# One load of 128 rows issued as sixteen loads of 15, 14, 13, ... 1 and 8 rows

## The chip, the cores and the metric

The kernel runs on one core of a Trainium2 chip. The time is device microseconds for one execution of the program; the median of three runs is given. The profile is one other execution, taken by the hardware profiler.

## The reference

A decode step for four sequences (one new token each, width 576): layer norm, attention over the last 4096 positions of a key/value cache (32 query heads of width 128 on 16 key/value heads), output projection and residual; then layer norm, a gated MLP of width 4608 with a ReLU gate, and residual. All inputs and the output are bf16.

```python
def _A_ref(x, k_cache, v_cache, wq, wo):           # Hq = 32, Hkv = 16, Sk = 16384, Dh = 128
    W = min(4096, max(256, Sk // 4))
    q = (x @ wq).reshape(B, Sq, Hq, Dh).transpose(0, 2, 1, 3)
    k = jnp.repeat(k_cache[:, :, Sk - W:, :], rep, axis=1)
    v = jnp.repeat(v_cache[:, :, Sk - W:, :], rep, axis=1)
    p = softmax(jnp.einsum("bhqd,bhkd->bhqk", q, k) * Dh ** -0.5)
    o = jnp.einsum("bhqk,bhkd->bhqd", p, v)
    return o.transpose(0, 2, 1, 3).reshape(B, Sq, Hq * Dh) @ wo
def _B_ref(x, W_gate, W_up, W_down):               # W_gate, W_up: 576 x 4608, W_down: 4608 x 576
    gate, up = x @ W_gate, x @ W_up
    return (gate * (gate > 0) * up) @ W_down
h  = x + _A_ref(layernorm(x), ...)
h2 = h + _B_ref(layernorm(h), ...)
```

## The kernel before

The kernel is written engine by engine: each operation is put on the list of its engine by hand, with the operations that it depends on, and `Prog.emit` turns those into semaphore waits. An engine runs its list in order. All large loads are issued by SP (the sync queue), in the order of the program text; only the load of x and half of the output's store are issued by ACT.

**What is loaded, in order.** W_q (the last 64 of its 576 rows first, in one piece; then the other 512), then 16 K tiles and 16 V tiles of 4 MB each (one sequence and four key/value heads a tile), alternating from the fifth K tile on, then W_o, W_gate, W_up and W_down. The K and V tiles go through four slots of one big SBUF tensor, `arena`; the later weights are laid over the same space. `place` keeps, for each 64 columns of `arena`, which operation read them last (`owner`), and makes a load wait for that reader. So SP waits, before most loads, for matmuls that free the space. Each load has its own semaphore or that of its slot; a load adds 16 to it when it has landed in full.

**What is computed.** For each K tile: a transposition on DVE in place (L422), then the score matmuls on PE (L446 and, for those that reuse the loaded weights, the helper at L34). For each V tile: the matmuls of probabilities by values (L507, L34), and a selection of the wanted rows on ACT and DVE (L517, L520, L523, L524). After the last V tile: the output projection (L615, L34), the norm (L618 to L645), the gate and up matmuls (L664, L34), ReLU and product (L670, L673), a transposition (L677), the down matmuls (L685), two copies (L701, L702) and the store (L706).

**Around the change.** W_gate and W_up have 576 rows; 512 of them are loaded as 128 partitions of four rows each (`main_rows`), and the last 64 as 128 partitions of half a row each (`last_rows`): 2304 elements, 4608 bytes a partition. The loop at L268 to L277 issues, for W_gate, the last 64 rows (called part 4) at L276, then the 512 rows in one load; for W_up the last 64 rows, then three quarters of the others, then the last quarter. W_down comes in five pieces (L282) of 15, 10, 7, 3 and 1 of its 36 rows a partition. The load of W_gate's part 4 waits for nothing that the load of W_o before it did not wait for; the load after it waits for the matmuls of an earlier V tile. The gate matmuls (L664) read part 4 first.

```python
def last_rows(W):
    return W[512:576, :].rearrange("r (a n) -> (r a) n", a=2)
...
for g, W in ((0, B_W_gate), (1, B_W_up)):
    for m, n, src in ((4, F // 2, last_rows(W)), ...
        place(("gu", g, m), off, n, ("GU", g, m), lambda e, off=off, n=n, src=src: e.dma_start(out=arena[:, off:off + n], in_=src))
```

Of the kernel before, what the change touches and what calls it, by code (L numbers as in the profile page):

```python
# [120 lines left out]
def bass_sequential_preLN__sliding_block_cached__glu_gated_reglu__decode_kernel(  # L121
# [12 lines left out]
    with ExitStack() as es:  # L134
        cnt = [0]

        def sb(name, shape, dt):
            return es.enter_context(nc.sbuf_tensor("sb_" + name, shape, dt))

        P = Prog()  # L140
# [8 lines left out]
        arena = sb("arena", [128, AW], BF16)  # L149
# [66 lines left out]
        def place(name, off, size, reader, make, key=None):  # L216
            deps = []
            for blk in range(off // 64, (off + size) // 64):
                r = owner.get(blk)
                if r is not None and r not in deps:  # L220
                    deps.append(r)
                owner[blk] = reader
            semk = key or "d_" + "_".join(str(v) for v in name)
            P.dma("sync", ("L",) + name, make, semk, deps)
            land[name] = off

        ring = [(-1 - 2 * NTILE) % NSLOT]
# [7 lines left out]
        def add_kv(kind, g):  # L235
            b, qd = divmod(g, 4)
            s = ring_slot()
            off = slot0 + s * TILE
            cache = A_k_cache if kind == "K" else A_v_cache
            src = cache[b, 4 * qd:4 * qd + 4, SK - WIN:SK, :].rearrange("a (p t) d -> p a (t d)", p=32)  # L240
            place((kind, g), off, TILE, ("QK", g) if kind == "K" else ("PV", g),
                  lambda e: e.dma_start(out=arena[:, off:off + TILE], in_=src), key=f"slot{s}")  # L242


        def main_rows(W):
            return W[0:512, :].rearrange("(p r) n -> p (r n)", r=4)

        def last_rows(W):
            return W[512:576, :].rearrange("r (a n) -> (r a) n", a=2)

        P.dma("sync", ("L", "wq", 1), lambda e: e.dma_start(out=pT[:, 0:2048], in_=last_rows(A_wq)), "d_wq1")  # L251
        s = ring_slot()
        wq_off = slot0 + s * TILE
        place(("wq", 0), wq_off, TILE, "QMM",
              lambda e: e.dma_start(out=arena[:, wq_off:wq_off + TILE], in_=main_rows(A_wq)), key=f"slot{s}")  # L255
        for g in range(NTILE):
# [6 lines left out]
        for g in range(NTILE - 4, NTILE):  # L263
            add_kv("V", g)
        place(("wo",), WO_OFF, H * D, "WO",
              lambda e: e.dma_start(out=arena[:, WO_OFF:WO_OFF + H * D], in_=A_wo.rearrange("(p r) n -> p (r n)", p=128)))
        gu_off = {}
        off = WO_OFF + H * D  # L268
        for g, W in ((0, B_W_gate), (1, B_W_up)):
            for m, n, src in ((4, F // 2, last_rows(W)), (0, 3 * F, main_rows(W)[:, 0:3 * F]), (3, F, main_rows(W)[:, 3 * F:4 * F])):  # L270
                if g == 0 and m == 0:
                    n, src = 4 * F, main_rows(W)
                elif g == 0 and m == 3:
                    continue
                gu_off[(g, m)] = off
                place(("gu", g, m), off, n, ("GU", g, m), lambda e, off=off, n=n, src=src: e.dma_start(out=arena[:, off:off + n], in_=src))  # L276
                off += n  # L277
        WD_ROWS = (0, 15, 25, 32, 35, 36)
        wd_off = off
        for r0, r1 in zip(WD_ROWS, WD_ROWS[1:]):  # L280
            place(("wd", r0), wd_off + r0 * D, (r1 - r0) * D, ("DOWN", 1),
                  lambda e, r0=r0, r1=r1: e.dma_start(  # L282
                      out=arena[:, wd_off + r0 * D:wd_off + r1 * D],
                      in_=B_W_down.rearrange("(p r) n -> p (r n)", p=128)[:, r0 * D:r1 * D]))
# [18 lines left out]
                                                in_=c_qm[:, :, :].rearrange("p q (h j) -> p q h j", j=4),  # L303
# [4 lines left out]
                                                in_=to_v[:, :, :].rearrange("p n (k a) -> p n k a", a=4),  # L308
# [14 lines left out]
        for sg in range(2):  # L323
            pool(f"c_toq{sg + 1}", lambda e, sg=sg: e.affine_select(
                out=toq[:, :, :, :], in_=toq[:, :, :, :],
# [213 lines left out]
        def finish_o():  # L539
            for q in range(4):  # L540
                for qd in range(4):
# [17 lines left out]
                                              in_=bass.AP(tensor=e8, offset=0, ap=[[8, 128], [0, 4], [1, 8]])), ["c_e8", "c_selc0"])  # L559
# [47 lines left out]
        for a in range(8):  # L607
            for n in range(2):
                for j in range(4):
# [4 lines left out]
                    else:  # L614
# [6 lines left out]
                                             in_=bass.AP(tensor=psb, offset=512 + 224, ap=[[4096, 128], [1, 64], [0, 2]])), ["part1"])  # L621
# [27 lines left out]
        for g in range(2):  # L649
            for c in (4, 0, 1, 2, 3):  # L650
                part_ = c if c == 4 or (c == 3 and g) else 0
                for m in range(3):
                    for j in range(4):
                        first = m == 0 and j == 0 and (c in (0, 4) or part_ == 3)
                        deps = [("L", "gu", g, part_)] if first else []
# [20 lines left out]
        for i in range(2):  # L676
            dve(("HHT", i), lambda e, i=i: e.transpose(  # L677
                out=hhT[:, 576 * i:576 * i + 576].rearrange("p (r q) -> p r q", q=32),
                in_=bass.AP(tensor=pp, offset=3712 + 18 * i, ap=[[PPW, 128], [1, 18], [36, 32]])), [("HH", m) for m in range(3)])
# [12 lines left out]
        for r in range(36):  # L692
            for n in range(2):
                deps = []
# [9 lines left out]
        for n in range(2):  # L704
            lo, hi = ncol[n]
            P.dma(("sync", "scalar")[n], ("O", n), lambda e, n=n, lo=lo, hi=hi: e.dma_start(  # L706
                out=orow[:, lo:hi], in_=out_sb[32 * n:32 * n + 4, 0:hi - lo]),
# [31 lines left out]
```

## Time and profile before

| | |
|---|---|
| median of 3 runs | 378.08 us (378.05 to 378.56) |
| the profiled execution: its own time is its span, first to last instruction | 376.5 us |
| loaded from HBM | 159.58 MB, 424 GB/s over the span |
| busy | PE 209.2 us, DVE 227.6, ACT 53.8, POOL 10.7 |
| chain of waits, share by engine | DMA 62%, DVE 18%, PE 18% |
| granted TensorE clock, mean | 0.791 |
| W_gate's part 4: size; issue to landing | 576 KB; 27.2 us |

The profile's page gives busy times and shares of the span for each engine, the DMA queues with what they moved, and the chain of work that ended last. Queue 1 is SP's, queue 10 ACT's; queues 8 and 14 carry the program's instructions. The median of the runs is 1.6 us above the span of the profiled execution.

### The profile page before, as it was taken

What the parts mean: (1) busy time and instruction counts of PE and PEld (TensorE: products, weight loads), DVE (VectorE), ACT (ScalarE), POOL (GpSimd) and SP (SyncE); (2) the same over time, 40 slices, a digit from 0 to 9 for tenths busy, and PEclk for the clock granted to TensorE, in tenths of its full rate; (3) what the DMA queues carried; (4) which work ended last, traced back from release to release, by engine and by line L of the source; (5) the groups of instructions that cost most, each with busy time, mean ns of one, the idle gap of its engine ahead of it and who ended that gap; (6) DMA issues with size and microseconds to landing.
All of it is one profiled execution on the core that took longest, in us unless ns stands there. A gap on an engine that the chain in (4) does not pass through costs nothing.

```text
span 376.5 us, 2541 instructions
## 1 busy us (share of the span) xinstructions
PE 209.2 (56%) x1447; PEld 39.2 (10%) x694; DVE 227.6 (60%) x164; ACT 53.8 (14%) x84; POOL 10.7 (3%) x29
## 2 busy tenths in 40 slices
PE   0404443249919091749282844664555687776748
PEld 0000000001101010101010100110000101003305
DVE  3088878779292959584847778665659423342140
ACT  3093000211000114010101140101010401121010
POOL 8300000000000000000000000000000000000000
PEclk9975666659979687788778885968596989996688
DMA  8999999999999999999999999999999999999996
GB/s 335 446 435 432 413 446 446 425 411 446 444 421 414 443 444 421 414 446 446 421 413 446 446 418 421 438 446 418 425 439 446 413 432 435 430 423 426 437 414 263
DMA packets 6514, 159.74 MB, mean 424 GB/s; under 512 B 736, under 2 KB 872, under 8 KB 1512
## 3 DMA queue, kind: packets, MB, share of 16 engines
q1 hardware_dynamic: 6488, 159.58, 98.8%
q8 instruction: 8, 0.13, 0.1%
q10 hardware_dynamic: 16, 0.01, 0.0%
q14 instruction: 2, 0.02, 0.0%
HBM read 159.58 MB, written 0.00 MB: 424 GB/s over the span
## 4 chain that ended last, share of the span: by engine, by line
DMA 62%; DVE 18%; PE 18%; SPq 1%; issue 1%; ACT 0%
DMA sb_arena<-in_A_k_cache_dram 53%; DVE sb_arena L422 16%; PE psb L34 11%; DMA sb_arena<-in_B_W_down_dram 9%; PE psb L446 4%; PE psb L507 2%; DVE sb_o_tmp L520 1%; DVE sb_pp L485 1%; PE psb L685 0%; SPq L242 0%; PE psb L473 0%; SPq L282 0%; ACT sb_out_sb L702 0%; SPq L255 0%; SPq L251 0%
## 5 line engine op out<-in xcount | busy, mean ns | idle before, releaser
L422 DVE STREAM_TRANSPOSE sb_arena<-sb_arena 128x8192 f32<-128x8192 f32 (+1 forms) x19 | 139.9, 7365 | 66.5 <-DMA sb_arena<-in_A_k_cache_dram 66.5
L446 PE MATMUL psb<-sb_arena 128*32 128x512 bf16 x256 | 42.5, 629 | 119.1 <-DVE sb_arena L422 119.0
L34 PE MATMUL psb<-sb_arena,sb_pp 128*128 128x512 bf16 x382 | 105.2, 383 | 2.7 <-issue 2.6
L507 PE MATMUL psb<-sb_arena,sb_pp 128*128 128x512 bf16 x115 | 44.1, 383 | 8.9 <-DVE sb_o_tmp L520 8.9
L34 PE MATMUL psb<-sb_arena 128*32 128x512 bf16 x256 | 44.2, 649 | 0.0
L517 ACT COPY sb_o_tmp<-psb 32x512 f32<-32x512 f32 x32 | 18.5, 577 | 179.3 <-PE psb L34 179.1
L520 DVE TENSOR_TENSOR sb_o_tmp<-psb,sb_fm 32x512 f32<-32x512 f32 x32 | 21.7, 678 | 16.9 <-PE psb L34 16.4
L446 PEld LDWEIGHTS psb<-sb_arena 128*32 128x32 bf16 x256 | 9.6, 119 | 161.4 <-DVE sb_arena L422 132.2
L507 PEld LDWEIGHTS psb<-sb_arena,sb_pp 128*128 128x128 bf16 x128 | 12.6, 99 | 113.4 <-issue 113.4
L524 DVE TENSOR_REDUCE sb_o_sel<-sb_o_tmp 128x128 f32<-128x512 f32 x16 | 17.7, 1106 | 0.5
L465 ACT ACTIVATE sb_pp<-psb,sb_hx 128x1024 bf16<-128x1024 f32 x4 | 4.5, 1113 | 78.4 <-DVE sb_hx L462 78.4
L485 DVE TENSOR_TENSOR sb_pp<-psb,sb_m 128x1024 bf16<-128x1024 f32 x8 | 9.4, 1209 | 4.5 <-PE psb L473 4.5
L480 ACT ACTIVATE sb_pp<-psb,sb_m 128x512 bf16<-128x512 f32 x16 | 9.7, 692 | 14.8 <-PE psb L473 14.8
L523 DVE TENSOR_TENSOR sb_o_tmp<-sb_o_tmp,sb_fm 64x512 f32<-64x512 f32 x16 | 11.0, 690 | 0.5
L413 ACT COPY sb_arena<-sb_q_keep 32x256 bf16<-32x256 bf16 x8 | 9.7, 1452 | 0.1
L685 PE MATMUL psb<-sb_arena,sb_pp 128*32 128x352 bf16 (+1 forms) x72 | 7.6, 349 | 3.7 <-DMA sb_arena<-in_B_W_down_dram 3.6
L399 DVE CAST sb_pp<-psb 128x512 bf16<-128x512 f32 x1 | 2.4, 2426 | 11.3 <-PE psb L379 11.3
L468 DVE STREAM_TRANSPOSE sb_pp<-sb_pp 128x1024 bf16<-128x1024 bf16 x4 | 5.0, 1246 | 5.1 <-ACT sb_pp L465 5.1
L473 PE MATMUL psb<-sb_pp,sb_to_v 128*32 128x256 bf16 x64 | 4.3, 401 | 6.2 <-DVE sb_pp L468 6.2
L673 DVE TENSOR_TENSOR sb_pp<-psb,sb_pp 128x384 bf16<-128x384 f32 x3 | 1.5, 551 | 9.0 <-PE psb L664 9.0
L379 PE MATMUL psb<-sb_arena,sb_xnT 128*32 128x512 bf16 x16 | 2.6, 628 | 7.2 <-DMA sb_arena<-in_A_wq_dram 7.2
L664 PE MATMUL psb<-sb_arena,sb_hnT 128*32 128x384 bf16 x40 | 4.2, 405 | 3.9 <-DVE sb_hnT L645 2.0
(119 smaller groups left out, 88.1 us busy)
## 6 DMA issues: line engine op xcount, KB each, us to landing
sb_arena<-in_A_k_cache_dram SPq DMA_DIRECT2D x16, 4096.0 KB, 26.2
sb_arena<-in_A_v_cache_dram SPq DMA_DIRECT2D x16, 4096.0 KB, 28.5
sb_arena<-in_A_wo_dram SPq DMA_DIRECT2D x1, 4608.0 KB, 26.2
sb_arena<-in_B_W_gate_dram SPq DMA_DIRECT2D x1, 4608.0 KB, 29.3
sb_arena<-in_A_wq_dram SPq DMA_DIRECT2D x1, 4096.0 KB, 12.9
sb_arena<-in_B_W_up_dram SPq DMA_DIRECT2D x1, 3456.0 KB, 30.3
sb_arena<-in_B_W_down_dram SPq DMA_DIRECT2D x1, 2160.0 KB, 29.6
sb_arena<-in_B_W_down_dram SPq DMA_DIRECT2D x1, 1440.0 KB, 32.6
```

The source lines that it names most:

```text
L34: return e.add_instruction(mybir.InstMatmult(name=e.bass.get_next_instruction_name(), engine=mybir.EngineType.PE, ins=[e.lower_ap(rhs), e. ...
L413: act("QW", lambda e, i=i, q=q: e.copy(out=bass.AP(tensor=arena, offset=32 * i * AW + 2 * i + q, ap=[[AW, 32], [512, 16], [136, 4], [32, 4]]),
L422: dve(("TRA", g), lambda e: e.transpose(out=dst, in_=src), [("L", "K", g)] if lo == 0 else [])
L446: fn = lambda e, out_=out_, lhsT=lhsT, rhs=rhs, start=start, stop=stop: e.matmul(out_, lhsT=lhsT, rhs=rhs, start=start, stop=stop, skip_gr ...
L480: act(("EV", b, 0), lambda e, a=a: e.activation(out=bass.AP(tensor=pp, offset=2 * a, ap=[[PPW, 128], [8, 2], [32, 128], [1, 2]]), in_=bank ...
L485: dve(("EV", b, 1), lambda e, n=n: e.tensor_tensor(out=bass.AP(tensor=pp, offset=16 + 8 * n, ap=[[PPW, 128], [32, 128], [2, 4], [1, 2]]), ...
L507: fn = lambda e, lhsT=lhsT, rhs=rhs, k=k, j=j: e.matmul(bank[2 + j], lhsT=lhsT, rhs=rhs, start=(k == 0), stop=(k == 7), skip_group_check=True)
L517: act(("OSC", g), lambda e, j=j: e.copy(out=o_tmp[32 * j:32 * j + 32, 0:512], in_=bank[2 + j][32 * j:32 * j + 32, :]), [("PV", g), ("OSEL" ...
L520: dve(("OSD", g), lambda e, j=j: e.tensor_tensor(out=ot(32 * j, 32), in0=bank[2 + j][32 * j:32 * j + 32, :].rearrange("p (t d) -> p t d", ...
L523: dve(("OS", g), lambda e: e.tensor_tensor(out=ot(64, 64), in0=ot(64, 64), in1=fmb(64, 64), op=ALU.mult), [("OSC", g)])
L524: dve(("OSEL", g), lambda e: e.tensor_reduce(out=o_sel[:, qd, b, :], in_=o_tmp[:, 0:512].rearrange("p (t d) -> p d t", d=DH), axis=AX.X, o ...
L685: return lambda e: e.matmul(bank[n][32 * n:32 * n + 32, 0:hi - lo], lhsT=lhsT, rhs=w[:, lo:hi], start=start, stop=stop, skip_group_check=True)
```

## The change

The load of W_gate's last 64 rows (128 partitions of 4608 bytes) is issued as sixteen loads to consecutive partitions: 15 partitions, then 14, 13, and so on to 1, and at the end 8, which make 128. All sixteen add to the semaphore that the one load had, and the reader waits for 256 in place of 16. `place` takes a list of loads for this. Same bytes, same places; all other loads stay as they are, and no other engine's list changes.

```diff
-            P.dma("sync", ("L",) + name, make, semk, deps)
+            for one in make if isinstance(make, list) else [make]:
+                P.dma("sync", ("L",) + name, one, semk, deps)
             land[name] = off
...
                 gu_off[(g, m)] = off
-                place(("gu", g, m), off, n, ("GU", g, m), lambda e, off=off, n=n, src=src: e.dma_start(out=arena[:, off:off + n], in_=src))
+                cuts = [0, 128]
+                if g == 0 and m == 4:
+                    cuts = [0]
+                    for k in tuple(range(15, 0, -1)) + (8,):
+                        cuts.append(cuts[-1] + k)
+                place(("gu", g, m), off, n, ("GU", g, m), [lambda e, off=off, n=n, src=src, p0=p0, p1=p1: e.dma_start(
+                    out=arena[p0:p1, off:off + n], in_=src[p0:p1, :]) for p0, p1 in zip(cuts, cuts[1:])])
                 off += n
```

## The prediction

> **What bounds the kernel now.** I read the slices of the span first, then the DMA queues, then the chain of waits for the last 40 us, and then how the transfers are issued.
>
> ```profile
> DMA  8999999999999999999999999999999999999996
> GB/s 335 446 435 432 413 446 446 425 411 446 444 421 414 443 444 421 414 446 446 421 413 446 446 418 421 438 446 418 425 439 446 413 432 435 430 423 426 437 414 263
> ...
> q1 hardware_dynamic: 6488, 159.58, 98.8%
> q8 instruction: 8, 0.13, 0.1%
> ...
> q14 instruction: 2, 0.02, 0.0%
> ```
>
> The sixteen DMA engines are busy from the first slice to the last but one, at a level rate, and queue 1, on which SP issues all loads, has nearly all of it. The kernel is a stream of 159.6 MB; no engine's busy share matters beside that. Keep the ten instruction packets in mind: they are the program's own instructions, fetched by the same DMA engines.
>
> ```profile
> 337.39 0.33 SPq L282
> 337.72 0.04 issue
> 337.76 0.43 SPq L282
> 338.19 0.04 issue
> 338.23 34.60 DMA sb_arena<-in_B_W_down_dram
> 372.83 0.04 issue
> 372.88 1.86 PE psb L685 x19
> 374.74 0.02 issue
> 374.76 0.44 ACT sb_out_sb L702
> ```
>
> This is the end of the chain that ended last. W_down's third piece lands at 372.83; then come 1.86 us of matmuls, the copy of 0.44 us and the store. The end follows the landing of the last loads one for one.
>
> A load has landed when its slowest DMA engine has finished its share, and the trace's semaphore records tell how far apart the sixteen are. W_down's last piece has sixteen completions, from 372.52 to 374.26 us. The packet records give more: on one engine a packet starts 3 to 4 ns before the recorded end of the one before it, so they sort into sixteen chains, each with its eight rows of every 128-row load. A row of 32 KB takes 1.213 us on every chain. The chains drift apart because each instruction packet puts the one chain that carries it behind by 0.7 to 1.6 us, the next row's stretching included. The ten packets sit in ten different chains. The chains end (us):
>
> - 372.05, 372.11, 372.16, 372.40, 372.57, 372.70: no instruction packet
> - 373.23, 373.32: one instruction packet of 8 KB (at 237.0 and 126.4 us)
> - 373.57 to 373.86, eight chains: one instruction packet of 16 KB
>
> The kernel waits for the chain at 373.86. The mean of the sixteen is 0.72 us earlier: that is the most that any shift of rows between the engines can gain, since it moves no byte out of the stream.
>
> **Which engines get more.** The W_gate piece has 128 rows of 4608 bytes. Before, each engine has eight. If a transfer of k rows (k under 16) runs on engines 0 to k-1, the transfers of 15, 14, ... 1 and 8 give engines 0 to 15 in turn 16, 15, 14, 13, 12, 11, 10, 9, 7, 6, 5, 4, 3, 2, 1 and 0 rows. The trace supports the "k rows on k engines": x's 4 rows (queue 10, at 2.8 to 3.1 us) fall in four different chains and bring four completions. It does not number the engines. [...]
>
> I take the four chains of x to be the ones that every transfer of 4 rows or more uses, so the ones that gain most: 8, 7, 6 and 5 rows, in an order that I can't read. By the chains they end at 372.40, 372.57, 372.70 and 373.23. The last of these had the 8 KB packet at 237.0. (The first may be exchanged with the chain that ends at 373.32; the two ran within 1 ns of each other between 64 and 126 us.)
>
> **The sum.** A row of 4608 bytes is recorded at 179 ns, 175 net of the overlap. A transfer's closing semaphore packet is 9 ns, 6 net.
>
> - Of the four: the chain at 373.23 gets 5 to 8 rows, 0.87 to 1.40 us, and 12 to 15 more semaphore packets, 0.07 to 0.09. It ends at 374.18 to 374.72. The other three end at 374.19 at the latest (372.70 + 1.40 + 0.09).
> - Of engines 4 to 7 (4 to 1 rows more): a chain without an instruction packet ends at 372.9 or before, the one at 373.32 at 374.1 at most. One of the late eight would end between 373.7 and 374.6.
> - Engines 8 to 15 lose 1 to 8 rows, 0.17 to 1.40 us, and end before 373.7.
>
> So the new last chain ends 0.32 to 0.86 us behind 373.86, most likely the one of the four that had its 8 KB packet. The middle of its four places is 0.59; I take **+0.6 us**. All five W_down loads lie behind W_gate in every queue, so all their landings on that chain move by as much, and the PE waits for them move too.
>
> **What else the change adds.** SP issues fifteen transfers more. An issue without a wait takes 0.43 us with 0.04 between, as the chain's lines above show; sixteen end at 311.34 + 16 x 0.47 = 318.9.
>
> ```profile
> 310.96 0.33 SPq L266 DMA_DIRECT2D sb_arena<-in_A_wo_dram  x1
> 311.34 9.12 SPq L276 DMA_DIRECT2D sb_arena<-in_B_W_gate_dram  x2
> 320.50 9.06 SPq L276 DMA_DIRECT2D sb_arena<-in_B_W_up_dram  x3
> ```
>
> The second W_gate transfer starts at 311.34 + 9.12 - 0.33 = 320.13, where a wait for the matmuls of L34 ends. The fifteen issues lie in that wait with 1.2 us to spare: nothing. Were each 0.2 us longer, the big W_gate load and what SP has behind it (W_up, W_down) would be issued 2 us later; they land 27 to 35 us after their issue, so this still costs nothing.
>
> ```profile
> sb_arena<-in_B_W_gate_dram SPq DMA_DIRECT2D x1, 4608.0 KB, 29.3
> ...
> sb_arena<-in_B_W_gate_dram SPq DMA_DIRECT2D x1, 576.0 KB, 27.2
> ```
>
> The piece itself lands at 338.5, at most 1.5 later now, and its first reader (L664) starts at 353.56: nothing. No engine but SP gets, loses or moves an instruction.
>
> [...] First the row: the five W_down loads are issued back to back down to one of 144 KB, and in the chains the next transfer's first row follows the semaphore packet without a gap; a transfer costs a chain 6 ns. [...]
>
> The cost that no row bounds well is SP's instruction stream. It has 49 instructions in the trace and 64 after. I read the two 8 KB instruction packets as DVE's, which had started 53 of its instructions in the trace by 126.4 us, and ACT's, 63 by 237.0. SP stays under both now, and would have 62 by 339 us. One such packet more would set one chain back by 0.7 to 1.0 us (0.31 for the packet, the rest in the row behind it), or by nothing that counts if it falls on a chain with time to spare. I leave it out of the sum and put it in the rivals.
>
> Against the profiled execution's span of 376.5 the sum is 377.1. The median of the runs is 378.08, 1.6 above the span, and I carry the 0.6 over to it: **378.7 us**. About 0.2%, 0.76 us here, is what a measurement of this kernel can tell from no change, so this counts as no change, at its slower edge.
>
> **Rivals.**
>
> 1. *Slower: SP's own instruction fetch.* The 64 instructions make SP fetch 8 KB near 330 to 339 us. On one of the engines that gained rows this comes on top: 0.7 to 1.0 us on a chain that ends at 373.8 to 374.7, so 0.7 to 1.8 us slower, 378.8 to 379.9. On engines 10 to 15 it costs nothing. For it: both other streams fetched at such a count. Against: nothing shows where SP stands in its block. It decides if a third packet of queue 14 shows up and its chain ends last.
> 2. *Level or a little faster: the rows go to early chains.* If the packet at 237.0 was not on one of x's chains, the four end at 372.4 to 372.7 plus 0.9 to 1.5, so at 373.9 to 374.2: 0.0 to 0.3 us slower. If x's rows and these are numbered differently, the best pairing, the earliest chain with 8 rows more, the next with 7 and so on, makes the last end 373.6 (373.23 with two rows more): 0.26 us faster, 377.8. Against: at 237.05 the chain that fits best is one of the four, and the second best, 3 ns off, already had its packet.
> 3. *The transfers don't go to engines 0 to k-1.* If a transfer of fewer rows starts at a changing engine, the load stays about level and the time at 378.1, within 0.3. If odd counts run on one engine, engine 0 has 86 rows of the 128, 78 more than before: 78 x 0.175 = 13.7 us slower, 391.8. x's four chains for 4 rows say nothing on odd counts.
>
> **How the numbers follow.** Forecast (+0.3 to +0.9): 0.57. Rival 1: 0.23. Rival 2: 0.12. Rival 3: 0.08, most of it level. Of the forecast a quarter lies over +0.76, of rival 1 nearly all. Slower by over 0.2%: 0.14 + 0.22 + 0.03 from rival 3, and a little for late chains among engines 4 to 7: 0.42. Faster by over 0.2%: no pairing of rows and chains reaches it; 0.04 for chains that differ from the profiled execution's. Same: the rest, 0.54. The range from 378.0 to 379.4 holds the forecast, the lower two thirds of rival 1 and most of rivals 2 and 3's level cases, about 0.85; the forecast's own is 378.4 to 379.0.
>
> **What would show it.** Right: the gate piece as 128 packets of 4608 bytes in sixteen transfers, the semaphore packets 112 more (128 for 16); completions of W_down's last piece with one or a few chains alone at the end, at 374.6 to 375.1 for 374.26, and more chains early than now; the same PE, DVE and ACT rows. Wrong: completions closer together and none alone at the end (rival 2), a third packet on queue 14 (rival 1), landings of the gate piece spread by many microseconds (rival 3), or the second W_gate transfer issued later than its wait allows.

## The result, and the profile after

The changed kernel takes 381.54 us (381.27 to 381.82, 4 runs) against 378.08 before: ratio 1.0086, 95% interval 1.0074 to 1.0098. That is 3.46 us slower, where 0.6 was forecast and 1.3 was the end of the range.

The slices and the DMA queues of the page after:

```profile
DMA  8999999999999999999999999999999999999995
GB/s 331 441 441 438 398 431 441 441 427 400 440 441 441 435 433 403 434 441 441 438 429 403 438 441 441 427 431 414 438 441 433 427 427 424 437 310 413 428 421 243
...
q1 hardware_dynamic: 6600, 159.59, 98.7%
q8 instruction: 8, 0.13, 0.1%
...
q14 instruction: 2, 0.02, 0.0%
```

The sixteen engines are as busy as before in every slice but the last (5 tenths for 6), and queue 1 carries the 112 closing packets more that were forecast (6600 for 6488). But the 36th slice, 333 to 342 us, falls to 310 GB/s, where its counterpart before shows 423. The engines don't pause there (9 tenths busy); they are slow. The other slices carry about the same rate as before (398 to 441 GB/s for 411 to 446, the first and the last left out).

The windows of the trace show it more sharply (window; its length; busy us of PE, PEld, DVE, ACT, POOL; TensorE clock; DMA share; GB/s). First before, then after:

```profile
core 0: us, PE busy (x) PEld busy (x) DVE busy (x) ACT busy (x) POOL busy (x), PEclk, DMA share, GB/s
330.00:336.00 6.00, 5.66 (x26) 0.68 (x7) 1.86 (x3) 0.00 (x0) 0.00 (x0) 1.00 0.90 385
336.00:342.00 6.00, 2.76 (x35) 1.41 (x33) 3.07 (x4) 2.64 (x4) 0.00 (x0) 0.84 1.10 469
```

```profile
330.00:336.00 6.00, 4.44 (x21) 0.49 (x5) 3.09 (x4) 1.15 (x2) 0.00 (x0) 1.00 1.06 422
336.00:342.00 6.00, 5.13 (x24) 0.49 (x5) 0.82 (x2) 0.82 (x2) 0.00 (x0) 1.00 0.99 248
```

From 336 to 342 us, in which most of the piece's rows run (335.4 to 341.5), the stream moves 248 GB/s at a full DMA share. The chain of waits ends as before, 3.75 us later:

```profile
341.16 0.33 SPq L289
341.49 0.04 issue
341.53 0.43 SPq L289
341.96 0.04 issue
342.00 34.58 DMA sb_arena<-in_B_W_down_dram
376.58 0.04 issue
376.63 1.86 PE psb L692 x18
378.49 0.02 issue
378.51 0.44 ACT sb_out_sb L709
```

W_down's third piece lands at 376.58 (372.83 before); matmuls, copy and store behind it take what they took. So all of it lies in the stream. The packet and semaphore records of the two profiled executions give the account, each figure a mean over the sixteen engines:

- The piece's 128 rows of 4608 bytes take 303.8 ns each, 180.5 before: 128 x 123.3 / 16 = 0.99 us.
- The 36,864-byte rows of W_o and W_gate next to them, 1.37 us each before (one, behind an instruction packet, 1.86), reach 2.70 us, 36 of them over 1.45; all 256 together take 23.72 us for each engine against 21.92: 1.80 us.
- Closing packets: 0.51 us against 0.41: 0.10.
- The last completion of W_down's last piece lies 1.21 us behind the mean of its sixteen, 0.70 before: 0.51.

These make 3.40. The last completion moved from 374.26 to 378.01; 0.42 of this was there before the piece (the last V tile in the fourth slot landed at 316.01 on average, 315.59 before), which leaves 3.33. The 0.42 is not the change's: of two runs below whose piece comes by the same transfers (e2 and e7) one has it and one does not (316.04 and 315.66).

So the cost is rows that have become slow, the piece's own and, still more, those of other loads in flight beside them.

### The profile page after: what moved, and what is told of

Read it like the earlier page. It is cut to its first block, busy times and chain, and to the rows that moved or that the text cites. A ratio compares the mean times of both kernels' runs of the same rounds, so it can differ in the third digit from the quotient of the medians.

```text
span 380.2 us, 2571 instructions
## 1 busy us (share of the span) xinstructions
PE 214.1 (56%) x1462; PEld 38.9 (10%) x694; DVE 228.1 (60%) x164; ACT 53.8 (14%) x84; POOL 10.7 (3%) x29
## 4 chain that ended last, share of the span: by engine, by line
DMA 57%; PE 22%; DVE 20%; issue 0%; ACT 0%; SPq 0%
DMA sb_arena<-in_A_k_cache_dram 48%; DVE sb_arena L429 16%; PE psb L34 13%; DMA sb_arena<-in_B_W_down_dram 9%; PE psb L453 4%; PE psb L514 3%; DVE sb_o_tmp L527 1%; DVE sb_pp L492 1%; PE psb L480 1%; PE psb L692 0%; DVE sb_pp L475 0%; DVE sb_hx L458 0%; ACT sb_pp L472 0%; SPq L289 0%; ACT sb_out_sb L709 0%
## 5 line engine op out<-in xcount | busy, mean ns | idle before, releaser
L453 PE MATMUL psb<-sb_arena 128*32 128x512 bf16 x256 | 44.7, 639 | 120.1 <-DVE sb_arena L429 120.1
L34 PE MATMUL psb<-sb_arena,sb_pp 128*128 128x512 bf16 x384 | 107.5, 390 | 0.0
L514 PE MATMUL psb<-sb_arena,sb_pp 128*128 128x512 bf16 x128 | 50.4, 394 | 8.9 <-DVE sb_o_tmp L527 8.9
L34 PE MATMUL psb<-sb_arena 128*32 128x512 bf16 x256 | 45.7, 645 | 0.0
L453 PEld LDWEIGHTS psb<-sb_arena 128*32 128x32 bf16 x256 | 10.4, 119 | 162.3 <-DVE sb_arena L429 133.1
L34 PE MATMUL psb<-sb_arena,sb_hnT 128*32 128x384 bf16 x80 | 8.4, 506 | 0.0
L671 PE MATMUL psb<-sb_arena,sb_hnT 128*32 128x384 bf16 x40 | 5.2, 497 | 5.0 <-DMA sb_arena<-in_B_W_up_dram 3.0
## 6 DMA issues: line engine op xcount, KB each, us to landing
sb_arena<-in_B_W_gate_dram SPq DMA_DIRECT2D x1, 4608.0 KB, 29.3
```

The lines of the kernel that those rows point to most:

```text
L34: return e.add_instruction(mybir.InstMatmult(name=e.bass.get_next_instruction_name(), engine=mybir.EngineType.PE, ins=[e.lower_ap(rhs), e. ...
L453: fn = lambda e, out_=out_, lhsT=lhsT, rhs=rhs, start=start, stop=stop: e.matmul(out_, lhsT=lhsT, rhs=rhs, start=start, stop=stop, skip_gr ...
L514: fn = lambda e, lhsT=lhsT, rhs=rhs, k=k, j=j: e.matmul(bank[2 + j], lhsT=lhsT, rhs=rhs, start=(k == 0), stop=(k == 7), skip_group_check=True)
```

## The experiments

The runs use this edit, in which a transfer is a pair of slices (start, stop, step), of partitions of `arena` and of rows of the source; e0 has no edit, e7 adds semaphores, and e8 and e9 put it on another piece:

```diff
-                cuts = [0, 128]
-                if g == 0 and m == 4: ...
+                cuts = [((0, 128, 1), (0, 128, 1))]
+                if g == 0 and m == 4:
+                    cuts = CUTS
+                place(..., [lambda e, ...: e.dma_start(
+                    out=arena[d[0]:d[1]:d[2], off:off + n], in_=src[s[0]:s[1]:s[2], :]) for d, s in cuts])
```

What each gave; the rows are the piece's, in its profile. Each ratio is against the kernel before, run beside it (medians 377.93 to 378.28):

| run: CUTS | us | ratio and interval | ns a row |
|---|---|---|---|
| e1: 8 x 16 neighbours | 381.63 | 1.0090 (1.0072 to 1.0108) | 293.6 |
| e2: 8 x 16, 8 apart | 380.79 | 1.0069 (1.0055 to 1.0083) | 294.0 |
| e7: the same, own semaphores | 381.00 | 1.0084 (1.0070 to 1.0098) | 295.7 |
| e3: 8 x 16, neighbours in `arena` only | 381.21 | 1.0080 (1.0067 to 1.0092) | 298.1 |
| e4: 8 x 16, neighbours in the source only | 380.74 | 1.0061 (1.0049 to 1.0073) | 293.8 |
| e5: staircase, 8 apart | 381.13 | 1.0080 (1.0067 to 1.0093) | 303.3 |
| e6: 4 x 32, 4 apart | 377.99 | 0.9999 (0.9990 to 1.0007) | 178.8 |
| e12: 4 x 32 neighbours | 380.43 | 1.0069 (1.0057 to 1.0082) | 308.7 |
| e10: 4 x 16, 4 apart, and one of 64 | 380.68 | 1.0072 (1.0059 to 1.0086) | 299.4 |
| e11: 96, 21 and 11 | 381.07 | 1.0087 (1.0074 to 1.0100) | 326.0 |
| e13: 7 x 16, 7 apart, and 16 neighbours | 380.43 | 1.0067 (1.0053 to 1.0080) | 287.3 |
| e15: 8 x 8 below 64, one of 64 above | 380.39 | 1.0066 (1.0053 to 1.0079) | 270.8 |
| e16: 8 x 8 above 64, one of 64 below | 381.35 | 1.0089 (1.0075 to 1.0103) | 314.7 |
| e17: 8 x 8 below 64 alone | 378.00 | 0.9992 (0.9983 to 1.0001) | 178.4 |
| e18: 8 x 8 above 64 alone | 380.55 | 1.0054 (1.0041 to 1.0066) | 317.6 |

### Equal shares: neighbours or not, in SBUF or in the source

Eight transfers of 16 bring 16 closing packets each, 128 in all: by that every engine has its eight rows again, and nothing is shifted between engines.

```diff
+ CUTS = [((16*j, 16*j + 16, 1), (16*j, 16*j + 16, 1)) for j in range(8)]   # e1
+ CUTS = [((j, 128, 8), (j, 128, 8)) for j in range(8)]                     # e2
+ CUTS = [((16*j, 16*j + 16, 1), (j, 128, 8)) for j in range(8)]            # e3
+ CUTS = [((j, 128, 8), (16*j, 16*j + 16, 1)) for j in range(8)]            # e4
```

> The W_gate piece comes by eight transfers of 16 neighbouring partitions: every DMA engine has its eight rows as before, but one row of each transfer, and at any time the sixteen engines read neighbouring rows of HBM and write neighbouring partitions of SBUF. After the change the piece's rows took 242 ns on average for 180 before (8 rows: 0.5 us an engine, 0.99 summed over both pieces of 4608-byte rows) and the rows of the W_gate load behind it 1482 for 1370 (16 rows of that size with W_o's: 1.8 us). Theory S (rows to neighbouring partitions share a way into SBUF) and theory H (neighbouring rows of HBM are read at the same time and share a channel): both slow, 1 to 3 us over before, piece's rows over 250 ns. Theory K (a closing semaphore packet behind every row holds the next row up): slow too, 1 to 3 us. Theory R (only the number of rows on an engine counts, as the prediction had it): 0.04 us over before, rows at 180 ns.

> The W_gate piece comes by eight transfers of 16 partitions that are 8 apart, so each engine reads and writes the rows that I take it to have had before, one a transfer. S and H: as before within 0.2 us, rows at 180 ns, for no two engines are at neighbouring rows or partitions. K: as slow as the eight transfers of neighbouring partitions, 1 to 3 us over before. R: 0.04 us over before.

> Eight transfers of 16 rows: the rows are 8 apart in HBM and go to neighbouring partitions (so the piece's rows lie in other partitions than the matmuls expect). S: as slow as with both neighbouring, 1 to 3 us over before, rows over 250 ns. H: as before within 0.2 us, rows at 180 ns. K: slow in this as in all four. R: 0.04 us over before.

> Eight transfers of 16 rows: the rows are neighbours in HBM and go to partitions 8 apart (so the piece's rows lie in other partitions than the matmuls expect). S: as before within 0.2 us, rows at 180 ns. H: as slow as with both neighbouring, 1 to 3 us over before, rows over 250 ns. K: slow in this as in all four. R: 0.04 us over before.

All four cost 2.5 to 3.4 us, with rows of 294 to 298 ns. So most of the loss is there without any shift of rows, and it depends neither on neighbouring rows of the source nor on neighbouring partitions as such.

### Before again, the staircase spread, 32 at a time, and own semaphores

```diff
  # e0: the kernel before, no edit
+ CUTS = [(q, q) for j in range(8) for q in ((j, 8*(15 - j), 8), (j + 8*(15 - j), 128, 8))]   # e5: 15 and 1, 14 and 2, ... 8 and 8
+ CUTS = [((j, 128, 4), (j, 128, 4)) for j in range(4)]                                       # e6
  # e7: e2, each transfer with a semaphore of its own, the first reader waiting for all
```

> The kernel before, unchanged, for a trace from the chip on which the others of this call run. All theories: the piece's rows at 180 ns. What is asked is whether the K and V rows of the first 100 us take 1217 ns on average, as in the first profile, or 1220 to 1236, as in the five profiles since: in the second case the 0.5 us that those lost there belong to the session and not to the change.

> The changed kernel's sixteen transfers with the same counts of rows (15 and 1, 14 and 2, and so on to 8 and 8), the rows of a transfer 8 partitions apart. Same 128 closing packets as in the changed kernel and as in the four kernels with eight transfers of 16. Theory K (each closing packet beyond the sixteen of one transfer holds all engines up by some 0.024 us, 2.7 us for 112): 2.5 to 2.7 us over before for the packets, and on top what the shift of rows to the low engines costs, which the prediction put at 0.3 to 0.9: 2.8 to 3.6. If neighbouring partitions are a cost of their own in the changed kernel, this one is 0.5 us or more below it; if the shift of rows costs nothing, it is at 2.5, as the eight spread transfers of 16 were.

> Four transfers of 32 partitions that are 4 apart: each engine has its eight rows, two of each transfer, and 64 closing packets in all (48 more than before, where eight transfers of 16 had 112 more and cost 2.5 us). K with a cost for each packet: 48/112 of 2.5, 1.1 us over before. If the cost comes only where a packet follows every single row: about 0.1 us over before, rows near 180 ns.

> Eight transfers of 16 partitions 8 apart, each with a semaphore of its own, so that no semaphore gets more than 16 closing packets. If the packets wait for each other at one semaphore: as before within 0.3 us. If each closing packet costs, wherever it goes (K): 2.5 us over before, as with the one semaphore, rows near 290 ns.

The kernel before once more took 378.63 (one run), rows 180.5 ns. The staircase with spread partitions (381.13) is as slow as the one with neighbours (381.54), and own semaphores change nothing (381.00, 380.79 without). But four transfers of 32 cost nothing at all: 377.99 and rows of 178.8 ns, with 64 closing packets for 16. That took the ground from the price of a transfer as such, and left two readings: that a single row for each engine and transfer is slow, or that it matters which partitions a transfer takes.

### Size of the rows, and few packets

```diff
-                if g == 0 and m == 4:
+                if g == 0 and m == 0:          # e8: W_gate's 512 rows, 36,864 bytes each, as 8 x 16, 8 apart
+                if g == 1 and m == 3:          # e9: W_up's last quarter, 9216 bytes each, the same
+ CUTS = [((j, 64, 4),) * 2 for j in range(4)] + [((64, 128, 1),) * 2]        # e10
+ CUTS = [((0, 96, 1),) * 2, ((96, 117, 1),) * 2, ((117, 128, 1),) * 2]       # e11
```

> The W_gate piece comes by one transfer as before; the large W_gate load behind it (rows of 36,864 bytes, 1.37 us each) comes by eight transfers of 16 partitions 8 apart, so a closing packet follows each of its rows: 128 packets for 16. Theory K1 (a closing packet behind every single row slows all engines, whatever the row's size): the 4.7 MB at the 250 GB/s that the slow stretch had in place of 430, up to 8 us over before, and at least 2.3 if the cost is one for each packet. Theory N (it does so only if the row is short against the closing of a transfer, as 0.18 us is): as before within 0.2 us, rows at 1368 ns. A limit on closing packets a microsecond is not among the theories any more: the four transfers of 32 closed 34 in a microsecond at full speed, the slow stretches 20 to 36.

> The W_gate piece as before; the last quarter of W_up (rows of 9,216 bytes, 0.35 us each) comes by eight transfers of 16 partitions 8 apart. The bytes between two closing packets on an engine are those of the four transfers of 32 (two rows of 4,608), which cost nothing. K1: 2.3 us or more over before, rows over 0.5 us. N with a limit set by the time or the bytes between two closing packets: as before within 0.2 us, rows at 0.35.

> The W_gate piece comes by four transfers of 16 partitions (one row an engine each) and one of 64 (four rows an engine): 80 closing packets, 64 of them behind a single short row. K1 and N both: about half of what eight such transfers cost, 1.0 to 1.4 us over before, the 64 single rows near 290 ns, the others at 180. If the slowing needs more than a few such transfers in a row, nothing.

> The W_gate piece comes by transfers of 96 partitions (six rows an engine), 21 (if they go to engines 0 to 6: three rows each) and 11 (engines 0 to 10, one each): ten rows on engines 0 to 6, seven on 7 to 10, six on 11 to 15. By the prediction's arithmetic, with engines 0 to 6 among those that end early: the last chain 0.17 us earlier than before, less up to 0.2 us for the eleven single rows: 0.2 us faster to level, and the completions of W_down's last piece 1.0 to 1.4 us apart from first to last, for 1.7 to 2.0. If low engines are the late ones: 0.35 us slower and the completions over 2 us apart.

The large rows slow down too: 390.57 (ratio 1.0337, 1.0322 to 1.0352), 2.71 us a row for 1.37. The middle ones: 382.06 (1.0106, 1.0090 to 1.0122), 640 ns a row for 352. The windows of the run with large rows:

```profile
348.00:354.00 6.00, 3.19 (x22) 2.83 (x18) 1.99 (x13) 0.20 (x1) 0.00 (x0) 0.89 1.08 242
354.00:360.00 6.00, 0.82 (x12) 0.00 (x0) 0.00 (x0) 0.00 (x0) 0.00 (x0) 0.50 0.84 174
360.00:366.00 6.00, 3.73 (x48) 0.74 (x20) 0.00 (x0) 0.00 (x0) 0.00 (x0) 0.50 1.01 388
```

From 336 to 360 us, while these rows (336.3 to 361.4) are in the stream, its windows of 6 us read 267, 203, 242 and 174 GB/s, about half of its rate; in the third line they end. Loads that come by one transfer as before slow down beside them: the rows of W_gate's piece took 248.9 ns and those of W_up's 292.2, for 180. Two runs lost more than any theory had set, e8 with 12.6 us (8 at most) and e10 with 2.7 (1.0 to 1.4); e11, by the prediction's arithmetic level or faster, lost 3.1. With three transfers, 48 closing packets at most where the 64 of e6 cost nothing, the piece (e11, 381.07) is as slow as with sixteen (381.54). So it is neither the closing packets nor the size of a row, and the theories that blamed these fall; single rows, and where the rows go, were left.

### Which partitions

Three theories of that kind could be told apart: that it counts how many different parts of the partition range a transfer reaches (P), that it counts whether an engine writes the partitions that it writes in a transfer of 128 (E), and single rows (C), once more without other differences. By P and E 32 neighbours should be as slow as 16 were, by C level. By P the 16 that lie 7 apart should be much faster than the other transfers of 16, by E and C as slow. By E the half below 64 in eights (e15) should be at least 0.8 us faster than its mirror image (e16), by P and C the same within 0.3. E needs an assignment of partitions to engines for this; the one that it used is the author's assumption, and no trace shows it.

```diff
+ CUTS = [((32*j, 32*j + 32, 1),) * 2 for j in range(4)]                              # e12
+ CUTS = [((j, j + 106, 7),) * 2 for j in range(7)] + [((112, 128, 1),) * 2]          # e13
+ CUTS = [((j + 32*i, 32*i + 32, 4),) * 2 for i in (0, 1) for j in range(4)] + [((64, 128, 1),) * 2]   # e15
+ CUTS = [((j + 32*i, 32*i + 32, 4),) * 2 for i in (2, 3) for j in range(4)] + [((0, 64, 1),) * 2]     # e16
```

> Four transfers of 32 neighbouring partitions in place of the four of 32 partitions taken 4 apart (which cost nothing: 377.99, ratio 0.9999, rows of 4608 bytes 178.8 ns). Transfers, rows for each engine (2 of each transfer), closing packets (64) and SP instructions are the same; only the partitions of a transfer differ. Three theories. [...] C: what counts is how many rows an engine has of each transfer (one is slow, two are not). P and E: rows of 4608 bytes near 294 ns and about 2.3 us slower, as with 16 partitions (380.3, ratio 1.006). C: level (378.0, rows 179 ns).

> [...]

> Partitions 0 to 63 by eight transfers of 8 partitions taken 4 apart (0, 4, ... 28; 1, 5, ... 29; and so on to 35, 39, ... 63), and partitions 64 to 127 by one transfer of 64. [...] C: single rows of 8 transfers are slow: the same as the mirror image within 0.3, 380.0 up.

> The mirror image: partitions 64 to 127 by eight transfers of 8 partitions taken 4 apart, and partitions 0 to 63 by one of 64. [...] E: at least 0.8 us slower than its mirror image: 380.0 up. P and C: the same as the mirror image within 0.3 us.

The four transfers of 32 differ in nothing but which partitions, with their rows of the source, make up a transfer, and cost 2.5 us as neighbours (380.43) and nothing 4 apart (377.99). From 336 to 342 us their windows read, 4 apart and then neighbours:

```profile
336.00:342.00 6.00, 4.09 (x19) 0.39 (x4) 1.83 (x3) 1.85 (x3) 0.00 (x0) 1.00 1.04 441
```

```profile
336.00:342.00 6.00, 2.76 (x35) 1.47 (x33) 3.07 (x4) 2.64 (x4) 0.00 (x0) 0.83 1.06 320
```

C is out. P is out by the 16 that lie 7 apart: they cover the range almost evenly and were slow all the same, 287 ns and 2.5 us. E forecast that the two mirror images differ, and they do, by 0.96 us; but the better one, 380.39, is 0.9 us over the 379.5 that E gave it at most. The packet records show the time: rows are at 178 to 182 ns at first, and again from 336.6 to 337.0, and mostly at 250 to 370 in between and after that (455 at most). Which row belongs to which transfer the records don't tell, so two more runs left the transfer of 64 out.

### The two halves alone

```diff
+ CUTS = [((j + 32*i, 32*i + 32, 4),) * 2 for i in (0, 1) for j in range(4)]   # e17: partitions 0 to 63
+ CUTS = [((j + 32*i, 32*i + 32, 4),) * 2 for i in (2, 3) for j in range(4)]   # e18: partitions 64 to 127
```

> The eight transfers of 8 partitions on partitions 0 to 63 alone; the transfer of 64 that followed is left out, so partitions 64 to 127 of this piece of W_gate are not loaded and the output lacks them. [...] Rival F (any transfer that does not cover the whole range of partitions, or that gives an engine a single row, slows what is in flight): rows of 250 ns or more, 0.8 us slower or more, the same as its mirror image.

> [...] Counts of transfers, rows and closing packets by engine are the same as in the run beside it. [...] F: the same as its mirror image within 0.3 us.

Their windows, the low half and then the high half:

```profile
330.00:336.00 6.00, 4.39 (x20) 0.49 (x5) 3.09 (x4) 1.16 (x2) 0.00 (x0) 1.00 1.05 451
336.00:342.00 6.00, 5.21 (x25) 0.49 (x5) 0.74 (x2) 0.74 (x2) 0.00 (x0) 1.00 0.99 422
```

```profile
330.00:336.00 6.00, 4.39 (x20) 0.49 (x5) 3.08 (x4) 1.16 (x2) 0.00 (x0) 1.00 1.03 392
336.00:342.00 6.00, 4.28 (x20) 0.39 (x4) 1.64 (x3) 1.66 (x3) 0.00 (x0) 1.00 0.89 234
```

The two have the same number of transfers, of rows and of closing packets, and eight partitions in each transfer in the same pattern; only 64 is added to each number of a partition and of its row in the source. One streams at 422 GB/s, its 64 rows at 178.4 ns (185 at most) and no larger row over 1.38 us; the other at 234, its rows at 317.6 ns and 40 of the 94 rows of 36,864 bytes that start between 330 and 342 us over 1.45 us, up to 2.57. In time 378.00 against 380.55. F is out, and of the theories E, which had forecast the low half at 377.6 to 378.2 and the high half at least 0.8 us slower, is what the runs leave standing. Shown is the pattern of the times: eight transfers of 8 partitions that lie 4 apart cost nothing below 64 and 2.5 us above it. Which engine writes which partition no trace shows, so E stays the author's reading.

No variant was faster than the kernel before beyond what the intervals allow.

## Why the prediction was wrong

**The step that failed** is the price of a row in "The sum": "A row of 4608 bytes is recorded at 179 ns, 175 net". It was measured on rows of 128-partition transfers and used for sixteen transfers of 15 to 1 and 8 neighbours; there a row took 303.8 ns, and the rows of W_o and W_gate beside it lengthened as well. That is 0.99 + 1.80 us of the 3.33, and the sum had nothing for it; no rival had it either. All of the 128 rows count, not only those shifted: the equal shares of 8 x 16 (e1 to e4) lose 2.2 to 2.4 us in the same two terms. The price itself was right where the rows kept their speed. With 64 rows left out (low half), the mean completion of W_down's last piece came 57.26 us behind that of the last V tile in place of 57.97: 0.71 less, where 64 x 0.175 / 16 gives 0.70.

**What the sum did not ask** is which partitions a transfer takes. Rows of 4608 bytes kept their speed in transfers of 32 partitions that lie 4 apart (178.8 ns) and of 8 that lie 4 apart below 64 (178.4). They did not as 32 neighbours (308.7), as 16 in any arrangement tried (287.3 to 298.1 where all eight transfers had 16), or as 8 that lie 4 apart above 64 (317.6). How much of the partition range a transfer reaches does not order these: 16 that lie 7 apart, over almost all of it, were slow, and 8 over a quarter of it were fast below 64 and slow above. E orders them only by the author's assumed assignment, and no run shows that: the trace names neither engine nor partition of a packet.

**The price of a transfer as such** was low, as "a transfer costs a chain 6 ns" had it: four transfers for one cost nothing (0.9999, 0.9990 to 1.0007), and neither did eight that brought 64 closing packets for 16 (0.9992, 0.9983 to 1.0001). What decided the price here was not the number of the transfers, but the partitions that they take.

**The shift between the engines** was about the right size, or somewhat smaller. In the changed kernel the last completion lies 1.21 us behind the mean, in the other staircase 1.33; with equal shares (e1 to e4, e7) it is 0.81 to 0.95, in the two profiles of the kernel before 0.70 and 0.84. That is 0.3 to 0.6 us, where the sum moved the last chain by 0.59. That all sixteen transfers start at the same engine, so that four of the chains get 5 to 8 rows more, is a term of the sum that no run shows; the runs showed only this spread. Which chain ends last, and with how many rows of the piece, is not settled: in the slow stretch a packet no longer always starts within 3 to 4 ns of the end before it, and the packets can be sorted in more than one way. The last chain ends at 377.55, and three more end within 0.25 us. In the medians the term is not settled either, each against the kernel before beside it: the staircase spread 8 apart lost 3.17 us, equal shares 8 apart 2.51 (e2) and 3.04 (e7), the changed kernel 3.46 and the equal shares of neighbours 3.35, with intervals that overlap.

**What else was right.** SP's timeline after:

```profile
313.42 10.84 SPq L282 DMA_DIRECT2D sb_arena<-in_B_W_gate_dram  x17
324.31 9.03 SPq L282 DMA_DIRECT2D sb_arena<-in_B_W_up_dram  x3
341.16 6.23 SPq L289 DMA_DIRECT2D sb_arena<-in_B_W_down_dram  x5
```

The sixteen issues end at 319.1, for 318.9 in the sum, partly by luck: they begin 2.1 us later than before, and take 0.25 to 0.47 us each where the sum had 0.43. The load of the other W_gate rows is issued 3.8 us later than before, after its wait for the matmuls of L34 (the kernel before in its second profile, e0, also issues it 3.3 us later, at 323.43), and lands 29.3 us after its issue, as before:

```profile
sb_arena<-in_B_W_gate_dram SPq DMA_DIRECT2D x1, 4608.0 KB, 29.3
```

The low half alone issues it as late (323.99) and loses nothing, so this was free.

**The rivals.** 1: queue 14 carries two packets as before; SP fetched nothing more by then. 2: no gain and no level outcome. 3: the sixteen transfers brought 128 closing packets, one for each row, odd counts too, as k engines for a transfer of k rows would bring. (Its 86 rows need even counts cut down as well, 14 to 2 engines and 12 to 4; with odd counts alone on one engine, engine 0 would have 72.)

**Open.** That the slow rows slow the loads beside them too, and for longer than their own bytes need, was seen (1.80 us beside 0.99 in the changed kernel), but its cause was not taken apart. A shift of rows between the engines without slow rows was not run, so the size of that term rests on the spread of the completions. Which row of a transfer goes to which engine no trace shows, and so not E either. Whether the partition or the row of the source counts is argued only: in the runs without the loss (e6 and e17) partition and row have the same number, and the two that part them (e3 and e4) have transfers of 16, which were slow with the same numbers too (e1 and e2). For the partition speaks that loads of other tensors, which share the partitions but not the source, slow down too (in e8 W_up's rows of 4608 bytes took 292.2 ns beside W_gate's). And the 0.42 us that some executions lose in their first 100 us was not pursued.

## What to carry to other kernels

In this kernel, whether cutting a 128-partition load in a stream queued 27 us ahead was free depended on the partitions of each cut: as 32 partitions 4 apart it took 377.99 us, as before; as 16 in any arrangement tried, or 32 neighbours, 380.4 or more. A cut that was not free took the whole stream from some 430 GB/s to 234 to 320 over six microseconds, the loads beside it too, so price such a cut by the stream's bytes in that stretch and not by its own. A row's duration in the trace is measured for its transfer's shape (180.5 ns here, 303.8 in the other shape): before using it for another shape, measure a row in that shape.

## What the runs showed of the hardware that was not expected

- Rows of 36,864 bytes, 1.37 us otherwise, took up to 2.9 us beside the slow rows of 4608 bytes (e5); when they came in transfers of 16 themselves (e8) a row took 2.71 us on average, and 174 to 267 GB/s of some 430 were left.
- SP's five last issues took 6.23 us where they took 2.23 before; the last alone took 4.43 us for 0.43. Nothing stood behind it, and its cause wasn't tried. It is not the loss: e12 lost 2.5 us with its last issue at 0.43.
- An issue on SP took longer with the partitions spaced out: 0.42 us for 32 neighbours (e12) and 0.59 for 32 that lie 4 apart (e6), 0.27 for 8 neighbours (the changed kernel) and 0.62 for 8 that lie 4 apart.
